# Running rows of an SSM branch: added to row 0 of the operands instead of one-row float32 products, in the first block of a fused layer

## The chip, the cores and the metric

The kernel runs on one core of one Trainium2 chip. The metric is the device time of one execution in microseconds. Before the change it is 493.52 us, the median of 3 runs (493.52 to 494.44).

A core has a matrix engine (TensorE, in the profile PE for products and PEld for loads of weights), three engines for elementwise work (VectorE or DVE, ScalarE or ACT, GpSimd or POOL) and a queue for transfers (SyncE or SP; ScalarE starts some transfers too). Each engine runs its own instructions in the order in which the program lists them, and waits at an instruction until what it needs is there. SBUF is the on-chip memory of 128 partitions, PSUM the memory that products are written to, in banks of 128 x 512 float32.

## The reference

A transformer-like layer over L = 2048 tokens of D = 448 channels: an adaptive layer norm, an SSM convolution along the tokens, a second adaptive layer norm, and a gated feed-forward part with F = 1792 hidden channels.

```python
x = A_u
mod = (_silu(c) @ w_mod).reshape(c.shape[0], 6, 1, -1)
sa, ca, ga, sb, cb, gb = (mod[:, 0], mod[:, 1], mod[:, 2], mod[:, 3], mod[:, 4], mod[:, 5])
h = _layernorm(x, axis=-1) * (1 + ca) + sa
x = x + ga * _A_ref(h, A_A_re, A_A_im, A_B_re, A_B_im, A_C_re, A_C_im, A_log_dt, A_Dskip)
h = _layernorm(x, axis=-1) * (1 + cb) + sb
x = x + gb * _B_ref(h, B_w_gate, B_w_up, B_w_down)
```

with

```python
# _A_ref: a causal convolution of h with K, and a skip
P = jnp.exp(logdA[:, :, None] * l[None, None, :])
K = jnp.einsum("dn,dnl,dn->dl", Cc, P, dB).real
...
y = y + u * Dskip[None, None, :]

# _B_ref
g = _silu(x @ w_gate)
u = x @ w_up
return (g * u) @ w_down
```

## The kernel before

**Tiles and blocks.** The 2048 tokens are 16 tiles of 128 tokens, one token per partition. They go through the feed-forward part in six blocks of 2, 2, 3, 3, 3 and 3 tiles. While TensorE works on one block, the other engines prepare the tiles of the next one. "The first block" is block 0 (tiles 0 and 1), within which tiles 2 and 3 are prepared; the prologue before it has made the rows and gates and has taken tiles 0 and 1 through the branch.

**The branch.** The exponents of the kernel K are so small that, after a test of their size, K is taken as a straight line in the distance of two tokens: K(t - s) = k0 + k1 (t - s), per channel. The convolution then is two sums over earlier tokens. For a tile, v0 = h * gm0 and v1 = h * gm1 (`s1`, two elementwise products, L824), where gm0 and gm1 hold k0, k1 and the output gate; the number of the token within its tile is worked into gm0. With `tri`, the 128 x 128 matrix of ones on and above the diagonal, as stationary operand, o = tri v0 and s = tri v1 are the running sums down the tile, and the branch adds o + tok * s to the residual (`s5`, L876 and L877). What the earlier tiles bring in is two running rows, run0 and run1, of 448 channels each: row 127 of s is the next run1, and 128 * run1 + row 127 of o the next run0 (L873 on ScalarE, L874 on VectorE). They come out in partition 127, and a small transfer from ScalarE's queue (L875) brings them to partition 0, where the next tile takes them.

They can enter a tile in two ways. A product of `tri[0:1, :]`, a single row of ones, with the running row adds it to every row of the sum; or the running row is added to row 0 of v0 and v1 ahead of the product, since row 0 goes into every running sum. The kernel before has the first way in the first block (`s4f`, L857 to L867: L861 is the product for s, in the reduced float32 format that TensorE takes in one pass; L862 the product for o in full float32, which is recorded as two matmuls; L863 and L864 are the one-row products, full float32 too). From the second block on it has the second way (`rows`, L827 to L830), there with v0 split into two parts for cheaper products (`s2`, `s4`).

**The order of work.** `ffn` runs 14 rounds per block, f = 0 to 13. A round is the gate and up products of one 128-wide slice of the hidden channels (L686, 22 matmuls) into two banks, silu on ScalarE (L701), the product of gate and up on VectorE (L714), its split into a high part (ScalarE, L717) and a low part (VectorE, L718), and then the down products of the slice before (L730). In the first block, the weights are split into a high and a low part on the way: w_gate and w_up by a cast on ScalarE (L120) and two subtractions on VectorE (L122, L124) two rounds ahead of their use, w_down by a cast (L112) and a subtraction (L114) in the round itself. Down products read the high part with the whole weight split, then the low part last.

The work on the next tiles is put between by hand, in slots: slot h belongs to round h // 2, ahead of the down products where h is even and behind them where it is odd. `TIMES` lists the slots; its first line is for block 0, with a list for tile 2 and one for tile 3, whose entries go one by one to the stages of `small_path` (the last of each list is the statistics of the second norm):

```python
((1, 1), 5, ((5, 10, 15, 15, 15), (9, 9, 18, 19, 19)), 19, (24, 23)),
```

So before the change tile 2 has `s0` at 5, `s1` at 10, `s4f`, `s5` and statistics at 15, and tile 3 `s0` and `s1` at 9, `s4f` at 18, `s5` and statistics at 19. On VectorE a slot's instructions stand behind the round's own: L114, L714, L122, L718, L124, then the slots. `s4f` also holds the skip product (L843) and the residual add (L866) on VectorE. Four PSUM banks go round among gate, up and s; o has a bank of its own, named cv in the profile. Tiles v0 and h are parts of one tile named m there, and v1 is v.

Of the kernel before, what the change touches and what calls it, by code (L numbers as in the profile page):

```python
# [29 lines left out]


TIMES = (
# [3 lines left out]
)  # L36
# [16 lines left out]
def f32(ap):  # L53
    return ap.bitcast(F32)
# [3 lines left out]
def tile_kernel(ctx, tc, x, a_re, a_im, b_re, b_im, c_re, c_im, log_dt, dskip,  # L58
                wd, wgate_up, states, groups, vecs, dft, idft, out):
    nc = tc.nc  # L60
    sy, ve, sc, po, pe = nc.sync, nc.vector, nc.scalar, nc.gpsimd, nc.tensor
# [10 lines left out]
    def bank():  # L72
        t = psg.tile([128, 512], F32, name="bank")
        return t
# [52 lines left out]
    tri = const.tile([128, 128], F32R)  # L127
# [3 lines left out]
    run0, run1 = run[:, 0, :], run[:, 1, :]  # L131
# [49 lines left out]
    def make_h(h, i, part=None, ca=ca1, sh=sa):  # L181
        m, rs = n1.of[i][0:2]
        if part != 1:
            ve.scalar_tensor_tensor(h, xs[i], m, ca, op0=OP.subtract, op1=OP.mult)
        if part != 0:
            ve.scalar_tensor_tensor(h, h, rs, sh, op0=OP.mult, op1=OP.add)  # L186
# [57 lines left out]
    with tc.tile_pool(name="pre", bufs=1) as pre:  # L244
# [6 lines left out]
        for kind, q in ((n[0], n[1:]) for n in ORDER.split()):  # L251
# [3 lines left out]
            elif kind == "m":  # L255
                g, b = int(q[0]), (slice(0, 2 * D), slice(2 * D, NM))[int(q[1])]
# [52 lines left out]
        for q in range(2):  # L309
# [14 lines left out]
        h01, v0, v1, hd, h2 = ([pre.tile([128, w], t, name=f"{n}_{q}") for q in range(2)] for n, t, w in  # L324
                               (("h", F32, D), ("v0", F32, D), ("v1", F32R, D), ("hd", F32, D), ("h2", F32, 512)))
# [482 lines left out]
    def small_path(pools):  # L808
        work = pools.work
        vs = {}  # L810

        def s0(i):
            h = h_of(i)
            make_h(h, i)
            vs[i] = h

        def s1(i, on_v=False):
            h = vs[i]  # L820
            v0 = v0_of(i)
            v1 = work.tile([128, D], F32R, name="v1", bufs=2)
            for v, g in ((v0, gm0), (v1, gm1)):
                (ve if on_v else po).tensor_tensor(v, h, g, op=OP.mult)  # L824
            vs[i] = h, v0, v1

        def rows(i, on_v=False):  # L827
            h, v0, v1 = vs[i]
            ve.tensor_tensor(v0[0:1], v0[0:1], run0[0:1], op=OP.add)  # L829
            (ve if on_v else po).tensor_tensor(v1[0:1], f32(v1[0:1]), run1[0:1], op=OP.add)  # L830

        def s2(i, on_v=False):
            rows(i, on_v)
            h, v0, v1 = vs[i]
            vh = work.tile([128, D], F32R, name="vh")
            vl = work.tile([128, D], F32R, name="vl")
            sc.copy(vh, v0)  # L837
            ve.tensor_tensor(vl, v0, f32(vh), op=OP.subtract)
            vs[i] = h, vh, vl, v1

        def s3(i, on_v=False):
            h = vs[i][0]
            (ve if on_v else po).tensor_tensor(h, h, gd, op=OP.mult)  # L843

        def s4(i):
            h, vh, vl, v1 = vs[i]
            o = CV[:, 0:D]
            s = bank()[:, 0:D]
            pe.matmul(o, tri, vh, start=True, stop=False)  # L849
            pe.matmul(s, tri, v1, start=True, stop=True)  # L850
            pe.matmul(o, tri, vl, start=False, stop=True)  # L851
            ve.tensor_tensor(xs[i], h, xs[i], op=OP.add)
            vs[i] = o, s

        def s4f(i):  # L857
            h, v0, v1 = vs[i]
            o = CV[:, 0:D]
            s = bank()[:, 0:D]  # L860
            pe.matmul(s, tri, v1, start=True, stop=False)  # L861
            pe.matmul(o, f32(tri), v0, start=True, stop=False)  # L862
            pe.matmul(s, f32(tri[0:1, :]), run1[0:1], start=False, stop=True)  # L863
            pe.matmul(o, f32(tri[0:1, :]), run0[0:1], start=False, stop=True)  # L864
            s3(i, True)
            ve.tensor_tensor(xs[i], h, xs[i], op=OP.add)  # L866
            vs[i] = o, s  # L867

        def s5(i):
            o, s = vs.pop(i)  # L870
            if i + 1 < NT:
                e = slice(96, 128)
                sc.copy(run1[e], s[e])  # L873
                ve.scalar_tensor_tensor(run0[e], run1[e], 128.0, o[e], op0=OP.mult, op1=OP.add)  # L874
                sc.dma_start(run[0:1], run[127:128])  # L875
            ve.tensor_tensor(xs[i], xs[i], o, op=OP.add)  # L876
            ve.scalar_tensor_tensor(xs[i], s, tok, xs[i], op0=OP.mult, op1=OP.add)  # L877

        v = lambda g: lambda i: g(i, True)
        return lambda b: ((s0, v(s1), s4f, s5), (s0, v(s1), v(s2), v(s3), s4, s5),  # L880
                          (s0, s1, s2, s3, s4, s5))[min(b, 2)]

    def general_path(pools, y):
# [34 lines left out]
    with tc.If(rv > 0) as cond:  # L918
        with ExitStack() as es:
            pools = Pools(es)  # L920
            run_blocks(pools, small_path(pools))
# [62 lines left out]
```

## Time and profile before

| what | value |
|---|---|
| median of 3 runs | 493.52 us (493.52 to 494.44) |
| span of the profiled execution | 491.7 us, granted TensorE clock 0.995 |
| PE busy | 482.0 us (98%), 2759 instructions |
| DVE busy | 265.9 us (54%) |
| ACT busy | 161.3 us (33%) |
| POOL busy | 70.3 us (14%) |
| block 0, from its first product to its last down product | about 39 to 99 us |

The span runs from the first to the last instruction of the profiled execution, and the time of a run is longer by what lies around it: 493.52 - 491.7 = 1.8 us. The profile gives no separate run time for the profiled execution. A row of the timeline gives the start in the span, the length, the engine, the line, the operation, output <- inputs, shapes and count, and in brackets how long the engine stood idle before it and what released it.

### The profile page before, as it was taken

To read this page: it belongs to the slowest core of one execution; us is meant where nothing else is said; L and a number is where in the kernel's file an instruction comes from. 1 tells how busy PE (TensorE), PEld (TensorE's weight loads), DVE (VectorE), ACT (ScalarE), POOL (GpSimd) and SP (SyncE) were. 2 spreads that over 40 slices of the span, in tenths; PEclk is the share of its full clock that TensorE was granted. 3 is DMA by queue.
4 is the path that set the end of the run, shared out by engine and by line. 5 is a ranking of instruction groups with operands and counts; after the bars stand their busy time and mean duration, and the time that the engine had idled before them with its cause. 6 is when DMAs were issued, how large, how long until landed. Compare 5 with 4: busy or idle time off the path is not lost.

```text
span 491.7 us, 6939 instructions
## 1 busy us (share of the span) xinstructions
PE 482.0 (98%) x2759; PEld 452.5 (92%) x2759; DVE 265.9 (54%) x516; ACT 161.3 (33%) x348; POOL 70.3 (14%) x92
## 2 busy tenths in 40 slices
PE   8999999999999999999999999999999999999993
PEld 5659988999999999999999999999999999999992
DVE  4868999568886445634735553473465353221113
ACT  5665555622226112224412222521222161111110
POOL 2241001000010032411006140101541100000000
PEclk9999999999999999999999999999999999999998
DMA  8944752020000200000300000030000001000001
GB/s 309 404 165 159 232 188 86 15 95 1 0 3 21 75 1 0 2 1 2 98 15 1 2 0 2 2 112 1 0 2 1 1 0 57 0 1 0 1 0 64
DMA packets 11979, 26.04 MB, mean 53 GB/s; under 512 B 1825, under 2 KB 7842, under 8 KB 11938
## 3 DMA queue, kind: packets, MB, share of 16 engines
q1 hardware_dynamic: 11232, 25.33, 14.9%
q8 instruction: 23, 0.38, 0.3%
q10 hardware_dynamic: 706, 0.18, 0.2%
q14 instruction: 18, 0.15, 0.1%
HBM read 21.80 MB, written 3.67 MB: 52 GB/s over the span
## 4 chain that ended last, share of the span: by engine, by line
PE 97%; DVE 1%; ACT 0%; issue 0%; POOL 0%; POOLq 0%; DVEq 0%
PE bank L686 58%; PE dn L730 27%; PE bank L225 2%; PE bank L241 1%; PE bank L206 1%; PE dn L420 1%; PE bank L229 1%; PE cv L851 0%; PE cv L849 0%; PE bank L850 0%; PE cv L225 0%; PE bank L376 0%; PE bank L863 0%; PE cv L206 0%; PE cv L864 0%; PE dn L310 0%
## 5 line engine op out<-in xcount | busy, mean ns | idle before, releaser
L686 PE MATMUL bank<-hhi,gu 128*128 128x384 f32 (+1 forms) x1169 | 210.2, 319 | 0.0
L686 PEld LDWEIGHTS bank<-hhi,gu 128*128 128x128 f32 x1169 | 190.4, 188 | 3.1 <-issue 0.7
L686 PE MATMUL bank<-hlo,gu 128*128 128x384 f32 (+1 forms) x668 | 131.6, 319 | 0.0
L714 DVE TENSOR_TENSOR bank<-raw,bank 128x384 f32<-128x384 f32 (+1 forms) x69 | 36.9, 534 | 144.0 <-PE bank L686 128.6
L686 PEld LDWEIGHTS bank<-hlo,gu 128*128 128x128 f32 x668 | 109.7, 188 | 0.1
L717 ACT CAST phi<-bank 128x384 fp32r<-128x384 f32 (+1 forms) x83 | 36.8, 444 | 145.2 <-DVE bank L714 145.2
L701 ACT ACTIVATE raw<-bank 128x384 f32<-128x384 f32 (+1 forms) x70 | 32.8, 469 | 121.8 <-PE bank L686 115.4
L718 DVE TENSOR_TENSOR plo<-bank,phi 128x384 fp32r<-128x384 f32 (+1 forms) x83 | 42.5, 512 | 37.5 <-ACT phi L717 37.5
L730 PE MATMUL dn<-wdh,phi 128*128 128x448 f32 x224 | 60.4, 368 | 0.0
L730 PE MATMUL dn<-wdh,plo 128*128 128x448 f32 x224 | 60.2, 367 | 0.1
L730 PE MATMUL dn<-wdl,phi 128*128 128x448 f32 x224 | 59.9, 366 | 0.0
L730 PEld LDWEIGHTS dn<-wdh,plo 128*128 128x128 f32 x224 | 42.1, 188 | 3.9 <-DVE plo L710 0.4
L730 PEld LDWEIGHTS dn<-wdl,phi 128*128 128x128 f32 x224 | 42.1, 188 | 3.6
L730 PEld LDWEIGHTS dn<-wdh,phi 128*128 128x128 f32 x224 | 39.6, 188 | 1.7 <-ACT run L873 0.7
L824 POOL TENSOR_TENSOR m<-m,gm 128x448 f32<-128x448 f32 x9 | 11.1, 1237 | 64.9 <-DVE m L186 55.3
L165 POOL TENSOR_SCALAR rsb<-mvb 128x3 f32<-128x3 f32 (+2 forms) x7 | 1.9, 272 | 120.4 <-DVE mvb L149 120.4
L165 POOL TENSOR_SCALAR rsa<-mva 128x3 f32<-128x3 f32 (+1 forms) x6 | 1.4, 229 | 105.9 <-DVE mva L149 105.9
L120 ACT CAST gu<-raw 128x1024 fp32r<-128x1024 f32 x14 | 14.6, 1044 | 0.0
L758 POOL TENSOR_TENSOR x<-x,raw 128x448 f32<-128x448 f32 x1 | 1.1, 1129 | 91.2 <-DVE raw L757 91.2
L837 ACT CAST vh<-m 128x448 fp32r<-128x448 f32 x12 | 6.8, 567 | 22.3 <-DVE m L829 22.3
L830 POOL TENSOR_TENSOR v<-v,run 1x448 fp32r<-1x448 f32 x9 | 11.4, 1269 | 17.8 <-DMA run<-run 17.5
L225 PE MATMUL bank<-wm,cs 128*128 128x448 f32 x30 | 12.6, 550 | 0.0
(196 smaller groups left out, 426.8 us busy)
## 6 DMA issues: line engine op xcount, KB each, us to landing
raw<-in_B_w_gate_up_dram SPq DMA_DIRECT2D x14, 512.0 KB, 3.8
rawd<-in_B_w_down_dram SPq DMA_DIRECT2D x14, 224.0 KB, 3.9
x<-in_A_u_dram SPq DMA_DIRECT2D x12, 224.0 KB, 2.8
out_dram<-x SPq DMA_DIRECT2D x11, 224.0 KB, 1.9
wm<-in_w_mod_groups_dram SPq DMA_DIRECT2D x5, 448.0 KB, 8.1
wm<-in_w_mod_groups_dram SPq DMA_DIRECT2D x5, 336.0 KB, 7.9
rawd<-in_A_u_dram SPq DMA_DIRECT2D x4, 224.0 KB, 3.3
out_dram<-rawd SPq DMA_DIRECT2D x4, 224.0 KB, 1.9
```

The source lines that it names most:

```text
L120: sc.copy(wgu[j][:, :, 0:4, :], w)
L206: pe.transpose(ps[:, j * 128:(j + 1) * 128], xn[i][:, k * 128:(k + 1) * 128], ident)
L225: pe.matmul(ps[:, 0:D], cs[:, k:k + 1].to_broadcast([128, 128]), w[:, k * D:(k + 1) * D], start=k == 0, stop=False)
L686: pe.matmul(ps[s][:, 0:n], w[:, s, a], (hlo if lo else hhi)[:, k, 0:n], start=first and q == 0, stop=end and q == len(ka) - 1)
L701: sc.activation(p[:, 0:n], ps[0][:, 0:n], AF.Silu)
L714: ve.tensor_tensor(ps[1][:, 0:n], p[:, 0:n], ps[1][:, 0:n], op=OP.mult)
L717: sc.copy(hi[:, 0:n], ps[1][:, 0:n])
L718: ve.tensor_tensor(lo[:, 0:n], ps[1][:, 0:n], f32(hi[:, 0:n]), op=OP.subtract)
L730: pe.matmul(dn[q][:, 0:D], u[:, cs], v, start=f == 0 and z == 0, stop=f == NF - 1 and z == 2)
L824: (ve if on_v else po).tensor_tensor(v, h, g, op=OP.mult)
L830: (ve if on_v else po).tensor_tensor(v1[0:1], f32(v1[0:1]), run1[0:1], op=OP.add)
L837: sc.copy(vh, v0)
```

## The change

In block 0 the two one-row products per tile go, L861 and L862 each close their sums themselves, and `rows` is put into the list of stages of the first block, so that the running rows are added to row 0 of v0 (VectorE) and of v1 (GpSimd, since `rows` is called here without its second argument). Tile 2 has this step at slot 13, behind the down products of round 6, and tile 3 at slot 17, behind those of round 8. All other slots stay.

```diff
 TIMES = (
-    ((1, 1), 5, ((5, 10, 15, 15, 15), (9, 9, 18, 19, 19)), 19, (24, 23)),
+    ((1, 1), 5, ((5, 10, 13, 15, 15, 15), (9, 9, 17, 18, 19, 19)), 19, (24, 23)),
...
             s = bank()[:, 0:D]
-            pe.matmul(s, tri, v1, start=True, stop=False)
-            pe.matmul(o, f32(tri), v0, start=True, stop=False)
-            pe.matmul(s, f32(tri[0:1, :]), run1[0:1], start=False, stop=True)
-            pe.matmul(o, f32(tri[0:1, :]), run0[0:1], start=False, stop=True)
+            pe.matmul(s, tri, v1, start=True, stop=True)
+            pe.matmul(o, f32(tri), v0, start=True, stop=True)
             s3(i, True)
...
-        return lambda b: ((s0, v(s1), s4f, s5), (s0, v(s1), v(s2), v(s3), s4, s5),
+        return lambda b: ((s0, v(s1), rows, s4f, s5), (s0, v(s1), v(s2), v(s3), s4, s5),
                           (s0, s1, s2, s3, s4, s5))[min(b, 2)]
```

The function that is now called in block 0 as well:

```python
def rows(i, on_v=False):
    h, v0, v1 = vs[i]
    ve.tensor_tensor(v0[0:1], v0[0:1], run0[0:1], op=OP.add)
    (ve if on_v else po).tensor_tensor(v1[0:1], f32(v1[0:1]), run1[0:1], op=OP.add)
```

## Prediction, written before the result was seen

> **What bounds the kernel now.** I read the chain of waits first, as a whole and then in order of time around the two places where the changed function runs (the last two gate and up rounds before and after 68 and 77 us). Columns: start, length, engine, output tile, line, count.
>
> ```profile
> PE 97%; DVE 1%; ACT 0%; issue 0%; POOL 0%; POOLq 0%; DVEq 0%
> ```
>
> ```profile
> 67.27 1.23 PE dn L730 x6
> 68.71 0.75 PE cv L862 x2
> 69.46 0.94 PE bank L863 x2
> 70.41 0.75 PE cv L864 x2
> 71.16 2.77 PE bank L686 x22
> 73.93 1.22 PE dn L730 x6
> 75.14 2.57 PE bank L686 x22
> 77.92 0.75 PE cv L862 x2
> 78.67 0.94 PE bank L863 x2
> 79.62 0.75 PE cv L864 x2
> 80.37 1.41 PE dn L730 x6
> ...
> 88.14 1.23 PE dn L730 x6
> ```
>
> TensorE sets the end, and the pieces touch: each start plus its length is the next start, but for 0.21 us of L861 ahead of each L862. Four one-row products (L863 and L864, two recorded matmuls each) lie on that chain. Next I asked for the busy time of each engine over the rounds of block 0 (columns: length, then PE, PEld, DVE, ACT, POOL with counts, then the granted clock, DMA share, GB/s).
>
> ```profile
> 63.50:67.30 3.80, 3.80 (x29) 3.70 (x29) 3.74 (x8) 2.15 (x5) 0.00 (x0) 1.00 0.61 203
> 71.20:75.10 3.90, 3.90 (x30) 3.81 (x30) 3.69 (x8) 1.94 (x4) 0.00 (x0) 1.00 0.48 177
> 84.40:88.10 3.70, 3.70 (x29) 3.63 (x28) 2.82 (x6) 2.08 (x5) 1.58 (x4) 1.00 0.26 71
> ```
>
> VectorE is full too: 3.74 of 3.80 us and 3.69 of 3.90 us, and only by 84 us has it air again. GpSimd is empty there. So the change takes time from one full engine and gives work to another full one; the question is how far VectorE's order of work lets TensorE move ahead. These are rows of VectorE in that stage, in order of time:
>
> ```profile
> 63.79 0.62 DVE L824 TENSOR_TENSOR v<-m,g 128x448 fp32r<-128x448 f32 x1
> 64.33 0.62 DVE L114 TENSOR_TENSOR wdl<-rawd,wdh 128x448 fp32r<-128x448 f32 x1
> 64.86 0.42 DVE L714 TENSOR_TENSOR bank<-p,bank 128x256 f32<-128x256 f32 x1
> 65.19 0.95 DVE L122 TENSOR_TENSOR gu<-raw,gu 128x768 fp32r<-128x768 f32 x1
> ...
> 66.97 0.63 DVE L114 TENSOR_TENSOR wdl<-rawd,wdh 128x448 fp32r<-128x448 f32 x1
> ...
> 71.28 0.63 DVE L874 SCALAR_TENSOR_TENSOR run<-run,cv 32x448 f32<-32x448 f32 x1 [0.38 <-PE cv L864]
> ...
> 74.07 0.61 DVE L114 TENSOR_TENSOR wdl<-rawd,wdh 128x448 fp32r<-128x448 f32 x1
> 74.93 0.95 DVE L122 TENSOR_TENSOR gu<-raw,gu 128x768 fp32r<-128x768 f32 x1
> 76.24 0.42 DVE L124 TENSOR_TENSOR gu<-raw,gu 64x256 fp32r<-64x256 f32 x1
> 76.70 0.63 DVE L114 TENSOR_TENSOR wdl<-rawd,wdh 128x448 fp32r<-128x448 f32 x1
> 77.82 0.43 DVE L714 TENSOR_TENSOR bank<-p,bank 128x256 f32<-128x256 f32 x1 [0.50 <-ACT gu L120]
> ...
> 85.76 0.41 DVE L718 TENSOR_TENSOR plo<-bank,phi 128x256 fp32r<-128x256 f32 x1
> ```
>
> The reader is to see that VectorE ran from 64 to 77 us with one short pause, the 0.38 us ahead of L874, and that this pause was a wait for the very product (L864) that is removed.
>
> **What is removed.** Per tile, L863 0.94 us and L864 0.75 us: 1.69 us, for two tiles 3.38 us, all on the chain. The 0.19 us that follows a change of weights after a float32 product (2.77 against 2.57 for the round, 1.41 against 1.22 for the down products) stays: it is paid behind L862 instead of L864. This 3.38 us is the most that can be won. For tile 2 it comes in full if the row is in time: the round after it starts at 69.46 instead of 71.16, and TensorE stands before tile 3's L861 at 77.71 - 1.69 = 76.02 and before its L862 at 76.23.
>
> **What is added, and what one costs.** Per tile one VectorE add into row 0 of v0 (L829) and one GpSimd add into row 0 of v1 (L830). Both exist in later blocks:
>
> ```profile
> L829 DVE TENSOR_TENSOR m<-m,run x12: 579/606/622, 116.9 to 378.2; 1x448 f32<-1x448 f32 x12
> L830 POOL TENSOR_TENSOR v<-v,run x9: 1130/1142/1532, 180.3 to 374.3; 1x448 fp32r<-1x448 f32 x9
> 116.89 0.60 DVE L829 TENSOR_TENSOR m<-m,run 1x448 f32<-1x448 f32 x1
> 117.42 0.61 DVE L830 TENSOR_TENSOR v<-v,run 1x448 fp32r<-1x448 f32 x1
> ```
>
> On VectorE one row costs 0.60 us until its end and moves the next instruction by 0.53 us (117.42 - 116.89); that there is one partition instead of 128 saves nothing. On GpSimd it is 1.14 us alone and up to 1.53. GpSimd's queue is empty here, so its own time would be free, were it not for what the two engines do to each other. The next rows are from block 2, and the last is an undisturbed L838:
>
> ```profile
> 198.08 0.56 DVE L714 TENSOR_TENSOR bank<-raw,bank 128x384 f32<-128x384 f32 x1
> 198.66 1.15 POOL L824 TENSOR_TENSOR v<-m,g 128x448 fp32r<-128x448 f32 x1
> 199.66 0.62 DVE L829 TENSOR_TENSOR m<-m,run 1x448 f32<-1x448 f32 x1
> 199.76 1.53 POOL L830 TENSOR_TENSOR v<-v,run 1x448 fp32r<-1x448 f32 x1
> 200.97 0.82 DVE L838 TENSOR_TENSOR vl<-m,vh 128x448 fp32r<-128x448 f32 x1 [0.69 <-ACT vh L837]
> 118.13 0.62 DVE L838 TENSOR_TENSOR vl<-m,vh 128x448 fp32r<-128x448 f32 x1
> ```
>
> GpSimd's row began 0.10 us behind a VectorE row and lasted 1.53 instead of 1.14: it lost 0.39 us, until 200.15, which is 0.13 us before the VectorE row ended (200.28). L838 then began inside GpSimd's row and lasted 0.82 instead of 0.62: it lost 0.20 us, until 201.17, which is 0.12 us before GpSimd's end (201.29). So each holds the other off, the first one wins, and a GpSimd row closes VectorE for about 1.0 us (200.15 to 201.17). L714, with one operand in PSUM, kept 0.56 us beside GpSimd's 198.66 and its predecessor, so only adds with both inputs in SBUF are shut out: here L114, L122, L124 and the row itself. The Trainium skill, page "SBUF — State Buffer", section "Who interferes with whom", says the same as a rule: a VectorE instruction with two SBUF inputs and a GpSimd instruction that reads SBUF share one port pair, locked for the whole instruction by whichever starts first. The rows agree with it, 0.20 us and 0.39 us; it speaks against putting a GpSimd row beside a full VectorE.
>
> **Tile 2, step by step (row at slot 13).** v1 is written at 63.79 + 0.62 = 64.41, and GpSimd's row can start just after; but L114 has begun at 64.33, so GpSimd begins 0.14 before L114's end, at 64.81, and closes VectorE until 65.81. L714 (64.86) passes. L122, due at 65.19, waits for 65.81: 0.62 us lost. VectorE's own row stands behind L124, at 66.97 + 0.62 = 67.59, and ends at 68.19; TensorE wants it for L862 at 68.71. It is in time by 0.5 us, so the 1.69 us of tile 2 are won. VectorE is now late by 0.62 + 0.53 = 1.15 us, of which the removed pause gives back 0.38 (v0's product ends at 69.46, s is ready sooner, L874 waits for nothing): 0.77 us late at L874, which runs from 72.05 to 72.68. Behind it on ScalarE's queue stands the DMA of the running rows; silu and the casts of round 8 wait with it 0.77 us longer, which VectorE, itself late by as much, doesn't notice.
>
> **Tile 3 (row at slot 17).** The DMA of L875 in this place took
>
> ```profile
> run<-run ACTq DMA_DIRECT2D x1, 3.5 KB, 2.2
> ```
>
> so the rows land at 72.7 + 2.2 = 74.9, some tenths sooner at best. L114, before at 74.07, is due at 74.84. If it is first, GpSimd begins at 75.32 and closes until 76.32, and L122, due at 74.93 + 0.77 = 75.70, loses 0.62. If GpSimd is first (74.6), L114 loses 0.76. I take 0.7. VectorE's row stands behind the rest of round 8 (L718, then L124 at 76.24), in the place that L114 had: 76.70 + 0.77 + 0.7 = 78.17, end 78.77. TensorE has stood before L862 since 76.23. It goes on at about 78.85, plus 0.20 for weights that weren't loaded ahead: a wait of 2.82 us. GpSimd's row (at most 75.32 + 1.14 = 76.46) comes earlier than that and L861 hides in the wait. L862 then ends at 79.80 and the down products (1.41) at 81.21; before, 80.37 + 1.41 = 81.78.
>
> **The sum.** -3.38 + 2.82 = -0.56 us. The profiled span is 491.7 us, the median of the runs 493.52, so 1.8 us lie around the span; with them the forecast is 492.95, written 492.9.
>
> What is late next: behind its row VectorE stands 0.77 + 0.7 + 0.53 = 2.0 us later than before, and the old pause of 0.50 ahead of L714 (77.82) takes that to 1.5. The next reader to feel it is the last third of round 10's down products: its L718 ended at 85.76 + 0.41 and now at 87.67, the down products start at 88.14 - 0.56 = 87.58 and come to that third after two thirds of 1.23, at 88.40. That covers it with 0.7 us, so I cost it at nothing; with the cover gone, half a microsecond of more delay would show half as a wait there. The loads of weights stand three rounds ahead of their use and cost nothing.
>
> Bounds: if the two engines didn't hold each other off, the row of tile 3 would run from 76.70 + 0.53 - 0.38 = 76.85 to 77.45, the wait would be 77.53 + 0.20 - 76.23 = 1.50 and the gain 1.88. If each GpSimd row closed VectorE for the 1.53 us of its longest row, VectorE would lose up to 1.0 more in all and the time would be 0.5 above before.
>
> **The rivals.** *VectorE isn't held off* (gain 1.9, 491.6): for it, GpSimd reads one partition only; against it, L830 of 199.76 read one partition too and L838 lost 0.20. *Only one of the two rows falls on an add with two SBUF inputs* (gain about 1.2, 492.3): the meeting hangs on tenths of a microsecond at 64.4 and 74.9; against it, in both orders worked out above some add is shut out. *Slower, by the granted clock*: TensorE stands for 2.8 us, longer than anywhere in the middle of this trace, and comes back at a lower clock. At half the clock over one round and its down products (2.57 + 1.23) it loses 3.8 us more: 493.52 - 0.56 + 3.8 = 496.8; it turns slower than before from 0.56 us of loss on. Against it stands the prologue, where TensorE paused and the clock stayed at 1.00:
>
> ```profile
> 34.00:36.00 2.00, 1.64 (x5) 0.42 (x5) 0.62 (x3) 1.71 (x5) 0.00 (x0) 1.00 0.00 0
> ```
>
> though that pause was only 0.36 us of 2.00. The Trainium skill, page "TensorE: Matmul & The Clock Gate", Part 1, has the array fall to half rate after about 3.4 us of idleness; by that the wait is too short by 0.6 us, and no run shown here tests it. *The gain in full* (3.4, 490.1) would need VectorE's row by 76.2, and it stands behind L124, which even before ended at 76.66; I give it almost nothing.
>
> **How the numbers follow.** My forecast, both rows meeting VectorE and a gain of 0.1 to 0.95: 0.52. One meeting: 0.15. None: 0.16. Full gain: 0.02. Lower clock: 0.07. VectorE held off longer, or a wait behind round 10 that I cost at nothing, time from 0.1 below to 0.9 above before: 0.08. A measurement of this kernel tells 0.2%, 1.0 us, from no change. Faster by more: 0.16 + 0.02 + 0.14 of the one meeting + 0.04 from the forecast's edge = 0.36. Slower by more: 0.07 of the clock + 0.04 = 0.11. Within: 0.53. The range goes from 491.3, below the case without any meeting, to 494.2, half a microsecond's extra hold with the scatter of the runs (493.52 to 494.44) on it; it leaves out the full gain and the clock.
>
> **What would show it.** Right: no L863 or L864; TensorE's chain unbroken at tile 2 with its next round at 69.5; a pause of TensorE of 2.5 to 3 us ahead of tile 3's L862 whose releaser is VectorE's row at L829; an L122 near 65 us that lasts about 1.5 instead of 0.95, and an L114 or L122 near 75 us that lasts 0.6 longer; clock 1.00 after it. Wrong: L122 and L114 at their old lengths (then the gain is near 1.9), a pause of TensorE at tile 2, a pause released by GpSimd, or new pauses of TensorE after 82 us.

## The result and the profile after

| | before | after |
|---|---|---|
| median of 14 runs each | 493.52 us (493.15 to 494.44) | 493.94 us (492.92 to 495.18) |
| ratio after / before | | 1.0006, 95% interval 0.9999 to 1.0013 |
| span of the profiled execution | 491.7 us, clock 0.995 | 491.7 us, clock 0.996 |
| PE busy | 482.0 us | 479.0 us |

No difference beyond 0.2%. Taken against 493.52 us the interval reaches from 0.05 us less to 0.64 us more. The forecast was 492.9, the range 491.3 to 494.2.

TensorE lost 3.0 us of work, and the time didn't move. The chain of waits of the changed kernel, the rows that answer to those of before (start, length, engine, output, line, count):

```profile
65.24 2.57 PE bank L686 x22
67.81 1.23 PE dn L730 x6
69.04 0.21 PE bank L861
69.25 0.75 PE cv L862 x2
70.00 2.58 PE bank L686 x22
...
78.64 0.62 DVE m L829
79.26 0.04 issue
79.31 1.02 PE cv L862 x2
80.33 1.22 PE dn L730 x6
81.54 2.58 PE bank L686 x22
```

Tile 2 (69.04) is what was forecast: no L863, no L864, and round 8 follows at once. From the start of round 7 to the end of round 8 it took 72.58 - 65.24 = 7.34 us, before 73.93 - 64.71 = 9.22: 1.88 us less, 0.19 more than L863 and L864 by themselves. At tile 3 the chain leaves TensorE: between 72.6 and 79.3 it runs over ScalarE and VectorE, and its last piece ahead of L862 is VectorE's new row, L829. These are the rows of the timeline that carry it, VectorE, GpSimd, the transfer's start and TensorE's weight loads:

```profile
65.09 1.41 POOL L830 TENSOR_TENSOR v<-v,run 1x448 fp32r<-1x448 f32 x1 [17.29 <-DVE v L824]
65.72 1.58 DVE L122 TENSOR_TENSOR gu<-raw,gu 128x768 fp32r<-128x768 f32 x1
68.13 0.61 DVE L829 TENSOR_TENSOR m<-m,run 1x448 f32<-1x448 f32 x1
...
73.33 0.61 ACTq L873 DMA_DIRECT2D run<-run  x1
75.41 0.60 DVE L114 TENSOR_TENSOR wdl<-rawd,wdh 128x448 fp32r<-128x448 f32 x1
75.69 1.31 POOL L830 TENSOR_TENSOR v<-v,run 1x448 fp32r<-1x448 f32 x1 [9.20 <-DMA run<-run]
76.26 1.56 DVE L122 TENSOR_TENSOR gu<-raw,gu 128x768 fp32r<-128x768 f32 x1
77.06 0.19 PEld L861 LDWEIGHTS bank<-v,tri 128*128 128x128 f32 x1 [0.91 <-POOL v L830]
78.64 0.61 DVE L829 TENSOR_TENSOR m<-m,run 1x448 f32<-1x448 f32 x1
79.31 0.30 PEld L862 LDWEIGHTS cv<-m,tri 128*128 128x128 f32 x2 [2.06 <-DVE m L829]
```

In a row of PEld the bracket counts from the last load of weights; TensorE's products themselves stood still for 0.71 us before L861 and for 1.78 before L862. Each GpSimd row has its lengthened L122 beside it, 1.58 and 1.56 us instead of 0.95, and L862 waited for VectorE's row. Everything stands 0.53 to 0.54 us later than in the forecast, because this execution came out of its prologue that much later (round 7 at 65.24, before at 64.71).

To compare kernels without the prologue, I take one stretch throughout: from the start of round 7 to the start of the last, doubled down products of block 0. Before, that is 96.61 - 64.71 = 31.90 us; after, 96.38 - 65.24 = 31.14. The profiled execution thus won 0.76 us in block 0 and lost 0.53 in the prologue, and the median of the runs shows neither. Two questions were left: is the prologue's part chance, and why are the runs of the changed kernel spread over 2.3 us, those of before over 1.3? The list of executions has a hint for the second: 8 of the 14 changed ones have a mean granted clock of 0.992 to 0.994.

### The profile page after: what moved, and what is told of

Read it like the earlier page. It is cut to its first block, busy times and chain, and to the rows that moved or that the text cites. A ratio compares the mean times of both kernels' runs of the same rounds, so it can differ in the third digit from the quotient of the medians.

```text
span 491.7 us, 6931 instructions
## 1 busy us (share of the span) xinstructions
PE 479.0 (97%) x2751; PEld 451.2 (92%) x2751; DVE 268.0 (54%) x518; ACT 161.0 (33%) x348; POOL 73.1 (15%) x94
## 4 chain that ended last, share of the span: by engine, by line
PE 93%; DMA 2%; DVE 2%; ACT 1%; issue 0%; SPq 0%; ACTq 0%; DVEq 0%
PE bank L686 58%; PE dn L730 27%; PE bank L225 2%; DMA wm<-in_w_mod_groups_dram 2%; PE bank L206 1%; PE dn L420 1%; DMA vec<-in_c_log_dt_dram 1%; PE bank L229 1%; PE cv L849 0%; PE cv L851 0%; PE bank L850 0%; PE cv L225 0%; PE bank L376 0%; PE cv L862 0%; PE cv L206 0%
## 5 line engine op out<-in xcount | busy, mean ns | idle before, releaser
L714 DVE TENSOR_TENSOR bank<-raw,bank 128x384 f32<-128x384 f32 (+1 forms) x69 | 36.9, 535 | 144.2 <-PE bank L686 129.0
L717 ACT CAST phi<-bank 128x384 fp32r<-128x384 f32 (+1 forms) x83 | 36.9, 444 | 146.1 <-DVE bank L714 146.1
L830 POOL TENSOR_TENSOR v<-v,run 1x448 fp32r<-1x448 f32 x11 | 14.2, 1287 | 43.9 <-DMA run<-run 26.4
L122 DVE TENSOR_TENSOR gu<-raw,gu 128x768 fp32r<-128x768 f32 x13 | 13.5, 1043 | 0.0
```

What stands on the lines that cost most here:

```text
L122: en.tensor_tensor(lo, w[:, :, 0:3, :], f32(hi), op=OP.subtract)
L714: ve.tensor_tensor(ps[1][:, 0:n], p[:, 0:n], ps[1][:, 0:n], op=OP.mult)
L717: sc.copy(hi[:, 0:n], ps[1][:, 0:n])
```

## The experiments

All times are medians of executions on the chip of that comparison; "stretch" is the one defined above, from the one profile of each kernel, where before has 31.90.

| kernel | time, us | before there, us | ratio, 95% interval | stretch, us | executions under 0.995 clock |
|---|---|---|---|---|---|
| changed, again | 493.59 | 493.91 | 0.9981 to 1.0005 | 32.73 | 7 of 12 (0.992 to 0.994) |
| no GpSimd rows | 491.33 | 493.91 | 0.9935 to 0.9961 | 29.91 | 0 of 5 |
| no rows | 490.36 | 493.91 | 0.9910 to 0.9935 | 28.52 | 0 of 5 |
| all later | 495.01 | 493.91 | 1.0012 to 1.0033 | 31.71 | 11 of 11 (0.989 to 0.993) |
| before + GpSimd rows | 493.68 | 493.61 | 0.9995 to 1.0013 | 31.90 | 0 of 11 |
| tile 3 at slot 20 | 492.72 | 493.61 | 0.9977 to 0.9995 | 30.52 | 0 of 11 |
| the same, rows on VectorE | 492.75 | 493.61 | 0.9974 to 0.9992 | 30.35 | 0 of 11 |
| before, again | 494.00 | 493.61 | 0.9999 to 1.0017 | 31.90 | 1 of 11 (0.994) |
| tile 3 at slot 19 | 492.35 | 493.62 | 0.9963 to 0.9985 | 30.82 | 0 of 7 |
| the same, rows on VectorE | 492.42 | 493.62 | 0.9966 to 0.9983 | 30.65 | 1 of 11 (0.994) |
| rows and products | 495.58 | 493.62 | 1.0027 to 1.0065 | 33.05 | 3 of 8 (0.987 to 0.994) |
| rows and products, again | 496.75 | 493.62 | 1.0051 to 1.0091 | 33.06 | 4 of 6 (0.987 to 0.993) |

Of the 88 executions of before that ran beside these, 5 were at 0.994 and none lower.

### The changed kernel again

No edit.

> The changed kernel once more, unchanged, to see what in its profile and times comes back. In the first profile of it, block 0 from tile 2's entry to the last round was shorter by 0.77 us (TensorE's round 13 began at 92.94 instead of 93.17 although it came out of the prologue 0.54 us later), yet the runs' median is 0.42 us above before. Theory A (the prologue's 0.54 us is chance of the weight transfers): the new profile has the block-0 gain again, 0.6 to 0.9 us, with a prologue anywhere within 0.6 us. Rival B (the long wait of TensorE before L862 sometimes costs granted clock): executions with a mean clock of 0.992 or 0.993 come back, 1 to 2 us longer than those at 0.995 or 0.996, and more of them than with kernels that have no such wait. Rival C (the prologue is always later in the changed kernel): the prologue ends near 40.6 us again instead of 40.0.

Its profile caught what the times only hinted at. Busy times by window (length, PE, PEld, DVE, ACT, POOL, then the granted clock, DMA share, GB/s):

```profile
78.00:79.50 1.50, 0.22 (x1) 0.00 (x0) 1.44 (x4) 1.14 (x2) 0.00 (x0) 1.00 0.00 0
79.50:80.50 1.00, 0.50 (x1) 0.30 (x2) 1.00 (x3) 0.00 (x0) 0.00 (x0) 0.87 0.36 33
80.50:81.00 0.50, 0.50 (x3) 0.30 (x1) 0.50 (x2) 0.15 (x1) 0.00 (x0) 0.50 0.78 180
81.00:82.00 1.00, 1.00 (x3) 0.55 (x3) 1.00 (x2) 0.75 (x2) 0.00 (x0) 0.50 0.83 301
82.00:83.00 1.00, 1.00 (x5) 0.88 (x4) 0.94 (x3) 0.00 (x0) 0.00 (x0) 0.50 0.98 378
83.00:84.00 1.00, 1.00 (x6) 0.92 (x5) 0.93 (x3) 0.00 (x0) 0.00 (x0) 0.67 0.48 181
84.00:86.00 2.00, 2.00 (x19) 2.00 (x18) 1.90 (x4) 0.90 (x3) 0.00 (x0) 1.00 0.01 2
```

and its chain behind the wait:

```profile
80.00 1.65 PE cv L862 x2
81.65 2.19 PE dn L730 x6
83.84 2.57 PE bank L686 x22
```

The waits are those of the first profile (TensorE idle 0.69 us before L861 and 1.78 before L862, there 0.71 and 1.78), but here the clock goes to 0.50 just behind the start of L862, at 80.24, and is back by 84. From L862 to round 10 it takes 83.84 - 80.00 = 3.84 us instead of 81.54 - 79.31 = 2.23: 1.61 us lost, twice the 0.76 that the stretch had won. Rival B holds. Of twelve executions, the five at 0.995 or more have a median of 492.70, the seven below it 494.76. In the first comparison the same two groups lie nearer, 493.46 (six, 0.06 us below before) and 494.26 (eight), so the times show the win at full clock only to within about a microsecond. Theory A failed in this profile: the stretch is 0.83 us longer than before, though without the 1.61 us it would be 31.12, as in the first profile, and round 7 began 1.23 us later than before (65.94). Rival C is open until the profile of before is taken again.

Why the same waits cost the clock in one execution and not in another can be read from the traces, though no run was made to test it. Every profile ends with a fall of the clock too, once TensorE has no work left. These are two windows of the kernel before, the second one its end (the granted clock is the third number from the right):

```profile
120.00:480.00 360.00, 360.00 (x2036) 350.73 (x2036) 169.25 (x312) 96.80 (x198) 54.32 (x58) 1.00 0.04 14
480.00:491.70 11.70, 3.99 (x19) 3.04 (x17) 4.85 (x13) 0.80 (x3) 1.13 (x1) 0.81 0.21 67
```

Shorter windows of the same trace put the fall at 487.16, where the last product had ended at 484.06. In the profile with the lost clock the second fall, at 489.84, lies 409.60 us behind the first, 120 times 3.4133, and the low clock lasted 3.41 us. In the kernel "all later" below it lasted 3.41 us as well, and its two falls are 392.53 us apart, 115 times 3.4133 (falls and returns are read from windows of 0.05 us). So the clock seems to change only at instants 3.413 us apart; call the time between two of them a step. At the ends of the fourteen profiles the clock fell behind steps in which TensorE stood idle for 2.02 us or more, and stayed behind steps with up to 1.88 us.

The waits before L861 and L862, 2.47 us of idleness spread over 2.94 us, pass that mark only where they lie almost whole in one step. Here they do (76.83 to 80.24). In the first profile an instant lies at 78.10, counted back 120 steps from the fall at its end (487.70); it cuts the waits into 1.28 and 1.21 us, and the clock stayed. If the instants can lie anywhere, and the mark is taken at 1.95 us, the waits pass it by estimate in (0.47 + 0.52 + 0.52) / 3.41 = 44% of executions: a step is 0.47 us longer than the waits with what lies between them, and may miss 2.47 - 1.95 = 0.52 us of idleness at either end. At a mean clock of 0.993 or less were 13 of the 26 executions of the changed kernel, and none of the 88 of before. The mean clock counts the fall at the end too: in the profile of before taken again, the end alone brought it to 0.994, so 0.994 can mean either.

### Without GpSimd's rows; without any rows

```diff
-        return lambda b: ((s0, v(s1), rows, s4f, s5), ...
+        row0 = lambda i: ve.tensor_tensor(vs[i][1][0:1], vs[i][1][0:1], run0[0:1], op=OP.add)
+        return lambda b: ((s0, v(s1), row0, s4f, s5), ...
```

> The changed kernel without GpSimd's adds in block 0: the running row of v1 is left out for tiles 2 and 3. Theory (each GpSimd row shuts VectorE out of an add with two SBUF inputs for 0.6 us): both L122 that lasted 1.58 and 1.56 us are back at 0.95, TensorE's wait before tile 3's L862 shrinks by about 1.2 us to 1.2 to 1.5, and the time falls by 1.2 us against the changed kernel, to 1.6 to 2.0 below before. Rival (the longer L122 come from something else, VectorE's own row sets all): the L122 stay long or the wait stays at 2.3 to 2.6 us and the time stays within 0.4 us of the changed kernel.

```profile
65.74 0.95 DVE L122 TENSOR_TENSOR gu<-raw,gu 128x768 fp32r<-128x768 f32 x1
75.65 0.95 DVE L122 TENSOR_TENSOR gu<-raw,gu 128x768 fp32r<-128x768 f32 x1
78.08 0.30 PEld L862 LDWEIGHTS cv<-m,tri 128*128 128x128 f32 x2 [1.80 <-DVE m L878]
```

Both L122 are back at 0.95, L861 doesn't wait any more, and the stretch is 31.14 - 29.91 = 1.23 us shorter than in the changed kernel: two times 0.62. One pause of TensorE is left, 1.52 us of idle products, and no execution was under 0.995. The time fell by 2.58 us, the stretch by 1.99; the stretch is what was forecast, the other 0.6 isn't explained by it.

```diff
-        return lambda b: ((s0, v(s1), rows, s4f, s5), ...
+        return lambda b: ((s0, v(s1), lambda i: None, s4f, s5), ...
```

> The changed kernel without any running row in block 0 (neither VectorE's nor GpSimd's adds, so tiles 2 and 3 get nothing from earlier tiles). Theory (the four removed products were worth 3.38 us of TensorE, and the rows' place on VectorE takes most of it back): no wait of TensorE before L862, block 0 shorter by 3.2 to 3.4 us and the time 3.0 to 3.4 us below before. Rival (the products' time was hidden or VectorE's other work holds TensorE anyway): 1 us below before or less, with a new wait in rounds 8 to 11.

```profile
73.57 2.57 PE bank L686 x22
76.14 0.21 PE bank L861
76.35 0.75 PE cv L862 x2
77.10 1.24 PE dn L730 x6
78.34 2.23 PE bank L686 x19
```

```profile
84.81 0.30 PEld L730 LDWEIGHTS dn<-wdh,phi 128*128 128x128 f32 x2 [0.31 <-ACT phi L717]
```

No pause before L862. Round 10 starts 78.34 - 65.03 = 13.31 us behind round 7, before 81.78 - 64.71 = 17.07: TensorE is 3.76 us ahead, the 3.38 of the removed products and twice the 0.19 that stood behind L864. In round 11 the down products then wait for ScalarE's L717, which takes 0.38 of it back, a small case of the rival's new wait. So the stretch of 28.52, 3.38 us under before, meets the sum of the removed products by chance. The time is 3.55 us lower. The products were on the path in full, and the rest of what the changed kernel doesn't win is the cost of the rows on VectorE.

### GpSimd's rows alone, in the kernel before

```diff
-    ((1, 1), 5, ((5, 10, 15, 15, 15), (9, 9, 18, 19, 19)), 19, (24, 23)),
+    ((1, 1), 5, ((5, 10, 13, 15, 15, 15), (9, 9, 17, 18, 19, 19)), 19, (24, 23)),
...
-        return lambda b: ((s0, v(s1), s4f, s5), ...
+        spare_row = lambda i: po.tensor_tensor(run1[32:33], f32(vs[i][2][0:1]), run1[0:1], op=OP.add)
+        return lambda b: ((s0, v(s1), spare_row, s4f, s5), ...
```

> The kernel before with two extra GpSimd adds of one row (v1's row and the running row, written to a row of the run tile that nobody reads) at slots 13 and 17; the four one-row products stay, the output is the reference's. Theory (one GpSimd row by itself shuts VectorE out): L122 behind 64.4 us lasts 1.5 to 1.6 instead of 0.95, and another add near 75 us lasts about 0.6 longer; TensorE, which here comes to L862 1.7 us later per tile, isn't made to wait, so the time stays within 0.6 us of before and the clock stays at 0.995 or more. Rival (L122 was long because of VectorE's own row): all L122 of block 0 stay at 0.95.

```profile
64.83 1.38 POOL L880 TENSOR_TENSOR run<-v,run 1x448 f32<-1x448 f32 x1 [17.33 <-DVE v L824]
65.44 1.58 DVE L122 TENSOR_TENSOR gu<-raw,gu 128x768 fp32r<-128x768 f32 x1
...
75.11 1.14 POOL L880 TENSOR_TENSOR run<-v,run 1x448 f32<-1x448 f32 x1 [8.90 <-DMA run<-run]
75.45 1.62 DVE L122 TENSOR_TENSOR gu<-raw,gu 128x768 fp32r<-128x768 f32 x1
```

With nothing else changed, one GpSimd row of a single partition makes the VectorE subtraction beside it 0.63 to 0.67 us longer. The stretch is 31.90 and the time that of before: VectorE's lateness costs nothing as long as TensorE comes late itself. This is the rule of the Trainium skill, page "SBUF — State Buffer", section "Who interferes with whom", with its price in this kernel.

### The adding half alone

The rows at the slots of the changed kernel, with the four products left in, so that the running rows are added twice in block 0.

```diff
-    ((1, 1), 5, ((5, 10, 15, 15, 15), (9, 9, 18, 19, 19)), 19, (24, 23)),
+    ((1, 1), 5, ((5, 10, 13, 15, 15, 15), (9, 9, 17, 18, 19, 19)), 19, (24, 23)),
...
-        return lambda b: ((s0, v(s1), s4f, s5), ...
+        return lambda b: ((s0, v(s1), rows, s4f, s5), ...
```

> Only the adding half of the change: the rows of the changed kernel, at their slots, with the four one-row products left in (the running rows are added twice in block 0). Theory (the rows make VectorE's row of tile 3 end near 78.8, counted as in the profile of before, where TensorE now comes to L862 at 77.9): a wait of 0.9 to 1.3 us before tile 3's L862, time 0.7 to 1.5 us above before, clock 0.995 or more, since the pause is short. Rival (added rows are covered, the wait in the changed kernel has another cause): no wait, time within 0.4 us of before.

```profile
78.90 0.30 PEld L862 LDWEIGHTS cv<-m,tri 128*128 128x128 f32 x2 [1.17 <-DVE m L829]
```

At full clock it is as expected: the stretch 1.15 us longer, four executions at 494.54 to 494.87 with a clock of 0.997, some 1.0 us above before. But the others took 496.3 to 498.5, and that wasn't expected of a pause of 1.17 us (0.88 of idle products). A second run was to show the clock of such an execution:

> The rows with the products left in, once more (the running rows are added twice in block 0). In its first run the profile had a pause of 1.2 us before tile 3's L862 at full clock, and four of eight executions took 494.5 to 494.9 us at a mean clock of 0.997, but four took 496.3 to 498.5, three of them at 0.987 or 0.994. Theory (even this pause, followed by one-row products, sometimes costs granted clock): again two groups, and the longer executions at 0.994 or less; if the profile falls on one of them, the clock goes to 0.5 right behind the pause. Rival (the longer executions come from elsewhere, the prologue's transfers or that chip): all within 0.6 us of 494.7 here, or a profile of a long one with full clock behind the pause.

The two groups came back (494.42 at 0.997; 496.01 to 498.84 at 0.987 to 0.993, one of 495.40 at 0.995), but the profile fell on the execution at full clock again. The times go with the mean clock: from 0.997 to 0.987 is 0.010 x 495 = 5 us of full clock, about what three steps of 3.41 us at half clock lose, and the times differ by 4.4. So the loss is most likely one of granted clock here too, but where it lies in the execution, and why a shorter pause loses more, stays open. The pause stands next to the one-row products here; that these keep the clock up less than others do would be a guess, and in the kernel before, which has them without the pause, the clock stayed.

### Orders that spare TensorE the wait

```diff
-    ((1, 1), 5, ((5, 10, 13, 15, 15, 15), (9, 9, 17, 18, 19, 19)), 19, (24, 23)),
+    ((1, 1), 5, ((5, 10, 13, 16, 17, 19), (9, 9, 18, 22, 23, 23)), 23, (25, 25)),
```

> The changed kernel with the whole sums kept and later slots: tile 2's L861 and L862 at 16, its s5 at 17 and statistics at 19, tile 3's row at 18, L861 and L862 at 22, s5 and statistics at 23, the root at 23 and the normalised tiles at 25. Theory (TensorE only waits because it comes to L862 before VectorE's row; VectorE catches up by round 11): no wait of TensorE before L862, block 0 shorter by 3.0 to 3.4 us, time 2.8 to 3.4 us below before, and granted clock 0.995 or more in all executions if rival B of the first run is right. Rival (VectorE is the bound of block 0 as a whole): the wait only moves to a later round and the gain stays under 1.2 us.

The wait before L862 went, and a worse one came at the block's end. Timeline of TensorE's weight loads there, and two windows behind it:

```profile
94.04 0.14 PEld L206 LDWEIGHTS bank<-ident,raw 128*128 128x128 f32 x1 [2.13 <-ACT raw L199]
95.02 0.31 PEld L206 LDWEIGHTS bank<-ident,raw 128*128 128x128 f32 x3 [0.84 <-ACT raw L199]
...
96.08 0.20 PEld L206 LDWEIGHTS bank<-ident,raw 128*128 128x128 f32 x2 [0.54 <-ACT p L701]
```

```profile
96.00:97.00 1.00, 0.91 (x5) 0.88 (x6) 0.75 (x2) 0.25 (x2) 0.00 (x0) 0.94 0.00 0
97.00:98.00 1.00, 1.00 (x4) 0.87 (x3) 0.77 (x2) 1.00 (x4) 0.00 (x0) 0.50 0.00 0
```

The second norm of tile 3 now ends too late for the transposes of the next block. The clock goes to 0.50 behind this pause as well, and all 11 executions have a mean of 0.993 or less. The step that ends with the fall (93.47 to 96.88) holds only 1.52 us of idleness, and besides it mostly the transposes of L206; whether those count as work for the clock stays open. That the wait would move to a later round the rival had; the lost clock neither theory had.

```diff
-    ((1, 1), 5, ((5, 10, 13, 15, 15, 15), (9, 9, 17, 18, 19, 19)), 19, (24, 23)),
+    ((1, 1), 5, ((5, 10, 13, 15, 15, 15), (9, 9, 17, 20, 21, 21)), 21, (24, 25)),
```

> The changed kernel with tile 3's products at slot 20 instead of 18, its s5 and statistics at 21, the root at 21 and the normalised tiles at 24 and 25; tile 2 and both rows stay where they are. Theory (the wait before tile 3's L862 is taken away because TensorE comes there two rounds of its own later, and the late end of the norm, which cost 3 us in the last order tried, is two slots earlier): waits of TensorE in rounds 8 to 13 of 1 us in all or less, none long enough to cost clock; block 0 shorter by 2 to 3 us, time 1.8 to 3.2 below before and clock 0.995 or more in nearly all executions. Rival (VectorE holds TensorE at another place for as long): a wait of 2 us or more behind round 8 and a time within 1 us of before.

0.89 us below before, half of what I expected. TensorE no longer waits at L862, but waits of 0.66 and 0.70 us stand at round 8's down products, and others of 0.35 and 0.54 at the transposes: the rival's outcome, in pieces (a time within 1 us of before, waits that add up to over 2 us). None costs clock (0.995 to 0.998).

The same with both rows on VectorE (`v(rows)` in the list of stages):

> The same with both rows on VectorE, none on GpSimd. Theory (a GpSimd row costs VectorE 0.6 us by shutting it out, a second row on VectorE itself 0.53): the same time as with GpSimd's rows within 0.4 us, no L122 longer than 1.0. Rival (GpSimd's rows are free but for the two L122, or cost much more): a difference of over 0.6 us one way or the other.

492.75 against 492.72: as expected. A second row on VectorE costs it 0.53 us (the start of L830 less that of L829 in the prediction's rows), a GpSimd row 0.62.

Then the smallest edit of the changed kernel, one number:

```diff
-    ... (9, 9, 17, 18, 19, 19)), 19, (24, 23)),
+    ... (9, 9, 17, 19, 19, 19)), 19, (24, 23)),
```

> The changed kernel with one number altered: tile 3's products at slot 19 instead of 18, so that TensorE does round 9's down products (1.23 us) ahead of L861 and L862 instead of behind them. Theory (TensorE's waits of 0.7 and 1.8 us before L861 and L862 are VectorE's lateness, and a pause of 2.5 us in all sometimes costs granted clock): the wait shrinks by about 1.2 us to 1.0 to 1.5, the clock stays at 0.995 or more in nearly all executions, the time is 1.6 to 2.4 us below before. Rival (VectorE's lateness holds the down products of round 8 or 9 instead): the waits add up to 2 us or more again and the time is within 0.8 us of the changed kernel at full clock (about 0.8 to 1.2 below before).

```profile
77.62 0.30 PEld L730 LDWEIGHTS dn<-wdh,phi 128*128 128x128 f32 x2 [0.67 <-ACT phi L717]
79.02 0.30 PEld L730 LDWEIGHTS dn<-wdh,plo 128*128 128x128 f32 x2 [0.70 <-DVE plo L718]
80.12 0.30 PEld L862 LDWEIGHTS cv<-m,tri 128*128 128x128 f32 x2 [0.60 <-DVE m L829]
...
88.13 0.30 PEld L730 LDWEIGHTS dn<-wdh,phi 128*128 128x128 f32 x2 [0.73 <-ACT phi L717]
```

The waits add up to 2.70 us, as the rival had it, and the stretch, 30.82, is only 0.32 us better than in the changed kernel. The profiled execution is the slowest of the seven (494.06 us), since its round 7 began only at 66.04. Yet the median is 1.27 us below before, short of the theory's 1.6, and no execution was under 0.995: four pauses of 0.23 to 0.53 us of idle products instead of 2.5 us within 3 us. With both rows on VectorE:

> The same with both rows on VectorE. Theory: within 0.5 us of the last one, as in the pair before, since a GpSimd row costs VectorE 0.62 and a VectorE row 0.53; no L122 of over 1.0. Rival: over 0.6 us apart.

492.42, the same. These two are the fastest versions that leave nothing out, and they are faster than before (493.62); the intervals of both leave out no change. The changed kernel was not run in this comparison; in its own two it lay 0.42 above and 0.32 below before.

### Before again

> The kernel before once more, for its prologue and clock. Theory (the prologue's end is chance of the weight transfers): TensorE's second row of gates begins anywhere from 12.7 to 13.9 us as in the five other profiles; clock 0.995 to 0.997 in all executions, since TensorE has no wait over 1 us in it. Rival (the changed code makes the prologue later): it begins at 12.7 again.

In this profile the second row of gates began at 12.90 us (in the first of before 12.71; in the changed kernel's two profiles 13.25 and 13.96; with slot 20, which has the change in it, 12.70). In four of these five the products waited for the transfer of the gate weights, for 0.31 to 0.50 us, so the prologue's end depends on when these land, and C, which had it always later with the change, falls. That it is later on average isn't excluded: round 7 began at 64.71 to 64.96 in the three profiles without the change, and at 64.67 to 66.04 in the eleven others. The median of before again is 494.00 beside 493.61 of the same program: 0.4 us is about what such a comparison leaves uncertain.

## Why the prediction was right, and where it wasn't

**The steps on VectorE and GpSimd** hold, less the 0.54 us of the prologue. Tile 2's row was forecast from 67.59 and began at 68.13 - 0.54 = 67.59. L114 was due at 74.84 and came at 74.87, and L122 behind it lasted 0.61 longer (forecast 0.62). Tile 3's row was to end at 78.77 and ended at 79.25 - 0.54 = 78.71. L862 was to end at 79.80 and ended at 79.79. That an add with an operand in PSUM isn't held off shows here as well: the L714 that ran inside GpSimd's first row (65.39) took its usual 0.42 us. The one sign that I had named as speaking against it, a pause released by GpSimd, did appear: L861 waited 0.71 us for L830 until 76.5. The text had that end (at most 76.46) and hid it in the longer wait; it should have been named as an expected pause.

**The removed products** were worth 1.88 us per tile, 3.76 in all, not 3.38. The 0.19 us that I had kept, as paid behind L862 instead of L864, goes with the one-row products: behind L862 round 8 took 2.58 us and the down products 1.22, where behind L864 they had taken 2.77 and 1.41. At tile 2 TensorE only waits longer for it; the kernel without rows shows the 3.76.

**The sum** had -0.56 us at full clock; the stretch gave -0.76. The 0.2 us are the same gap at tile 3: I had charged the down products 1.41.

**The step that failed** is the rival "slower, by the granted clock", at 0.07, on the ground that a pause in the prologue had left the clock at 1.00. That pause was 0.36 us of 2.00 and said little about 2.5. A better row stood at the end of the same trace, where the clock fell 3.10 us behind the last product. In the runs it happens, by the mean clock, in 13 to 15 of 26 executions of the changed kernel (at 0.993 or less in 13, at 0.994 in two), at 1.61 us in the one that was profiled, not 3.8: a halved clock for some 3.4 us (by the windows above: 0.26 + 0.5 + 1 + 1 + 0.66). It joins the first case instead of replacing it. As an estimate of the mean, -0.76 + 13/26 x 1.61 = +0.05 us, or +0.17 with 15; the means of the two comparisons lie 0.34 above and 0.13 below before. So a time about that of before, and a good part of the spread, are accounted for; the rest is within the 0.4 us by which the same program differed. The Trainium skill, page "TensorE: Matmul & The Clock Gate", Part 1, has the fall after about 3.4 us of idleness; I had used that to call 2.8 us too short. Here it came after 2.5 us of idle products within 3 us, broken by L861, and not each time.

**Range and verdict** were right: no change that can be measured, 493.94 within 491.3 to 494.2. The point, 492.9, had the waits and left out the clock. That the range held all the same is partly luck: it was drawn without the clock, and the measured time fits in because the clock was lost in half of the executions and cost 1.6 us there instead of 3.8.

## What to carry to other kernels

A product taken off a full TensorE is won only as far as the engine that feeds it can follow: before moving work to a "free" engine, write down when the feeding engine's next row ends and when the consumer will now arrive. One long wait can cost more than the same wait in pieces, since the clock may fall behind it; here, moving the consumer one slot later broke the wait up, and a change that won nothing became one that wins 1.3 us. And an add on one partition is as long as one on 128 (0.61 and 0.62 us on VectorE, 1.14 and 1.15 on GpSimd), and on GpSimd it took 0.61 to 0.67 us out of each VectorE add with two SBUF inputs beside it.

## What the runs showed of the hardware

The granted clock was seen to halve behind 2.47 us of idle products within 3 us (in one of two profiles of the changed kernel; by the mean clock in 13 to 15 of its 26 executions) and behind idle products of 1.93, 0.65 and 0.30 us within 4.5 us, with transposes between (in the profile, and by the mean clock in 11 of 11). Both times it came back after 3.41 us. It seems to change only at instants 3.413 us apart, and to fall when TensorE stood idle for more than 1.9 to 2.0 us between two of them; this is read from the traces and was not tested by a run. Fitting that, no execution was under 0.995 behind one pause of 1.52 us (0 of 5) or four pauses of 0.23 to 0.53 us spread over 11 us (0 of 7; with both rows on VectorE one of 11, at 0.994). By the mean clock it fell in 7 of 14 executions of the kernel with rows and products, whose profiled pause is 0.88 us of idle products; that one isn't understood.
